# One first transfer, weights joined on VectorE in 16-bit steps, and a new order, in a convolution with two gated layers

## The chip, the cores and the metric

One core of one Trainium2 chip. The metric is the device time of one execution in microseconds; of several runs the median is given. TensorE is called PE, its weight load PEld, VectorE DVE, ScalarE ACT, GpSimd POOL, and the queue of SyncE, which issues most transfers, SP.

## The reference

The inputs are x (2 x 4096 x 192), eight rows of seven taps, and two pairs of matrices, 192 x 2048 and 2048 x 192.

```python
w = softmax(weight, -1)                       # 8 heads, 7 taps
x = causal_conv(x, w)                         # per head of 24 columns, over the sequence
h = x @ w_in                                  # first layer, 8192 x 192 @ 192 x 2048
P = a[0] + a[1] * h + a[2] * h2 + a[3] * h3
Q = 1.0 + np.abs(b[0]) * np.abs(h) + np.abs(b[1]) * h2
x = (P / (Q + 1e-06)) @ w_out
r = np.maximum(x @ w_in2, 0.0)                # second layer
out = (s * (r * r) + b2) @ w_out2
```

All of it is float32. The kernel keeps nearly float32 precision on PE by cutting operands into a high part (rounded to fp32r) and a low part (the remainder), with two or three products for one.

## The kernel before, in words

The 8192 tokens go in 16 blocks of 512, and the 2048 hidden columns in eight pairs of 128. For each block `x_path` convolves (`conv`, eight band matrices on PE), evacuates on ACT, transposes on PE and cuts the result into highs (ACT) and lows (DVE). `first` does one pair of the first layer: ten matmuls (`in1`, L383), then on ACT V, Q, R, Ln and Exp (L408 to L433), on DVE six steps (L419 to L450), on POOL one product (`lo`, L454), and on PE six and four matmuls (`out_high`, `out_low`, L392). `middle` turns the first layer's sums into the second's input, `second` does one pair of that layer (three steps on ACT, one on DVE, twenty matmuls), `finish` scales and stores. So a block has 8 pairs of each layer, and 8 `lo` products on POOL.

**Weights.** The matrices come as 64-bit integers (the float32 words, widened on the way in), 768 numbers wide and 16 tiles long: eight for the first layer, eight for the second. `load_raw` (L211, SP's queue) brings a tile of 767.8 KB. `convert` turns it into highs and lows:

- `masked` (DVE, L244) takes the sign off the top 16 bits, reading and writing every fourth 16-bit number
- `high` (ACT, L251) scales them into an integer tile z, `low` (ACT, L247) scales the lower word
- `sign` (DVE, L255) puts the sign back into every second 16-bit number of z
- `join` (POOL, L260) adds the two integer tiles, 768 wide, both in SBUF
- `highs` (ACT, L272 to L274) and `lows` (DVE, L278, L279, L282) cut the joined float into parts

**The start.** The taps come as 2 x 28 numbers (L670). Seven small steps on DVE and one on ACT make the softmax of them (L685 to L691), written with zeros around into one row per half of the heads. Eight transfers, four issued by SP and four by ACT (L697), spread that row into eight bands, 112 x 103 each, with a step of one number per partition. Coefficients a, b, s, b2 come in four further transfers on ACT's queue (L672, L702), each to 128 partitions. ACT's later instructions stand behind these issues in its own order. PE runs idle matmuls (`fill`, L659) meanwhile: 18 first, then 240 in the order, which must be done before block 0 of the second layer sums up.

**The order.** Every step is given to `Plan.order` with an engine, a cost, a due time (`when * PERIOD + KEY[name]`), the steps before it, and, for the steps marked `two` and for all of POOL, a lock that lets DVE and POOL not run at once. The planner picks for each engine the step of lowest due time among those that could start within WINDOW of the earliest. Steps are emitted in that order, so each engine and SP's queue has one fixed sequence; the waits between engines are semaphores.

Of the kernel before, what the change touches and what calls it, by code (L numbers as in the profile page):

```python
# [21 lines left out]
H, KS = 8, 7  # L22
# [16 lines left out]
PW = 3 * PC  # L39
VW = TR + TO - 1  # L40
MM = 0.2267
# [5 lines left out]

PERIOD = 29.4177
SAME, OTHER, WINDOW = 0.13, 0.18, 0.0816
KEY = {  # L50
    "B": -18.26, "Exp": 85.29, "Ln": 962.19, "S": -55.68, "Sq": 26.85, "V": -173.31,
    "add": -36.74, "again2": 92.78, "bias": -194.66, "conv": -113.91, "evac": -514.81,
    "f0": -183.70, "f1": -109.69, "fill": 1008.09, "finish": 1026.88, "flatten": 1223.69,
# [4 lines left out]
    "mid high": -118.59, "mid low": 106.79, "middle high": 7.19, "middle low": -60.45,  # L58
    "oh": 1243.60, "oh2": 1542.95, "ol": 20.35, "ol2": -329.62, "q": -163.53,
    "raw": -147.83, "relu": -68.11, "rest": -22.82, "rows": -471.89, "sign1": -269.27,  # L60
# [17 lines left out]
class Plan:  # L78
# [13 lines left out]
    def order(self):  # L92
# [23 lines left out]
        while len(out) < len(self.steps):  # L116
            first = None
            for engine, steps in ready.items():
                can = [(t, st) for t, st in ((start(st), st) for st in steps) if t is not None]
                if can:  # L120
                    t0 = min(t for t, _ in can)
                    t, st = min((c for c in can if c[0] <= t0 + WINDOW), key=lambda c: c[1].key)
                    if first is None or t < first[0]:
                        first = t, st
            t, st = first
            st.end = clock[st.engine] = t + st.cost
            if st.port:
                port[st.engine] = st.end
            if st.take:
                units = self.places[st.take]  # L130
                st.unit = min((u for u in units if units[u] is not None), key=units.get)
                units[st.unit] = None
            for holder in st.free:
                self.places[holder.take][holder.unit] = st.end
            ready[st.engine].remove(st)
            out.append(st)
            for d in users.get(st, ()):
                waits[d] -= 1
                if waits[d] == 0:
                    ready[d.engine].append(d)  # L140
# [4 lines left out]
def conv_rational_relu2(  # L145
    ctx: ExitStack,
    tc: tile.TileContext,
    xr: bass.AP,
    wr: bass.AP,
    w1: bass.AP,  # L150
    w2: bass.AP,
    a: bass.AP,
    b: bass.AP,
    s2: bass.AP,
    b2: bass.AP,
    out: bass.AP,
# [29 lines left out]
    ident = const.tile([P, P], F32, name="ident")  # L186
    band = const.tile([P, H, TO], F32, name="band")
    few = const.tile([P, 16], F32, name="few")
    ab, bb, babs, bias2 = few[:, 0:4], few[:, 4:6], few[:, 6:8], few[:, 8:10]
    ss, bs, lnb, exb, reb = (few[:, k:k + 1] for k in range(10, 15))  # L190
    ones = const.tile([P, 2], F32R, name="ones")
    qc = 1.0 + 1e-6

    def row(v):
        return bass.AP(v.tensor, v.offset, [[0, P], [1, v.shape[0]]])

# [34 lines left out]
    def convert(W, c, place, n, load):  # L231
# [8 lines left out]
        def masked(_):  # L240
            halves = raws[n].bitcast(U16).rearrange("p (n k) -> p n k", k=4)
            a["u"], a["top"] = halves[:, :, 3], halves[:, :, 2]
            a["y"] = raws[n].rearrange("p (n k) -> p n k", k=2)[:, :, 0]
            nc.vector.tensor_scalar(a["u"], a["top"], 0x7FFF, None, op0=ALU.bitwise_and)  # L244

        def low(_):
            nc.scalar.activation(a["y"], a["y"].bitcast(U32), AF.Copy, scale=2.0 ** -13)  # L247

        def high(tag):
            a["z"] = scratch(tag, I32, PW)  # L250
            nc.scalar.activation(a["z"], a["u"], AF.Relu, scale=2.0 ** 19, bias=reb)  # L251

        def sign(_):
            t = a["z"].bitcast(U16).rearrange("p (n k) -> p n k", k=2)[:, :, 1]
            nc.vector.scalar_tensor_tensor(  # L255
                t, a["top"], 0x8000, t, op0=ALU.bitwise_and, op1=ALU.bitwise_or
            )

        def join(_):
            nc.gpsimd.tensor_tensor(a["z"], a["z"], a["y"], op=ALU.add)  # L260

# [26 lines left out]

        s0 = st("masked", "DVE", 0.6, masked, (load,), two=True)
        s1 = st("low", "ACT", 0.8, low, (load, s0))  # L290
        s2 = st("high", "ACT", 0.85, high, (s0,), take="scratch")
        s3 = st("sign", "DVE", 0.93, sign, (s2,), two=True)
        s4 = st("join", "Pool", 1.84, join, (s1, s3))
        s5 = st("highs", "ACT", 1.35, highs, (s4, ("join", n - 1)))
        s6 = st("lows", "DVE", 1.05, lows, (s5,), two=True)
        st("weights", "DVE", 0.25, last_low, (s5, s6), free=(s2,), two=True)

# [12 lines left out]
    def x_path(blk):  # L310
# [339 lines left out]
    with tc.manual_schedule():  # L650
# [11 lines left out]

        fill(WARM)
        for n in range(FILLS):
            step("fill", n, "PE", 2 * MM, 0, lambda _: fill(2))

        small = tmp("Q", 3)[0:2].rearrange("p k n -> p (k n)")
        wt = small[:, 0:HH * KS].rearrange("p (h k) -> p h k", h=HH)
        mx = small[:, NB:NB + 3 * HH].rearrange("p (n h) -> p n h", h=HH)
# [21 lines left out]
        nc.vector.tensor_tensor(  # L691
            vv.rearrange("p (h n) -> p h n", h=HH)[:, :, TI - KS:TI],
            wt, each(mx[:, 2]), op=ALU.mult,
        )
        for h in range(H):
            v = vv[h // HH:h // HH + 1, h % HH * VW:(h % HH + 1) * VW]
            (nc.scalar, nc.sync)[h % 2].dma_start(  # L697
                out=band[:TR, h],
                in_=bass.AP(v.tensor, v.offset, [list(v.ap[0]), [1, TR], [1, TO]]),
            )  # L700
# [69 lines left out]
```

## Time and profile before

| | us |
|---|---|
| median of 3 runs | 1366.26 (1365.43 to 1367.29) |
| the profiled execution, its own time | 1367.33 |
| its span, first to last instruction | 1365.5 |
| PE busy | 1301.5 (95%) |
| DVE busy | 1222.5 (90%) |
| ACT busy | 1176.6 (86%) |
| POOL busy | 390.0 (29%) |

Busy time is a sum over stages that have different limits: PE's holds the idle matmuls of the start too. Which engine ends last is to be read stage by stage, from the view that cuts the span into stretches, and in the first 30 us from the timeline.

### The profile page before, as it was taken

How to read it: one execution, taken by the hardware profiler on the slowest of the kernel's cores; microseconds unless marked ns; L12 is line 12 of the kernel's file. 1: busy time of each engine (PE TensorE's matmuls, PEld its weight loads, DVE VectorE, ACT ScalarE, POOL GpSimd, SP SyncE). 2: the span in 40 equal slices, each digit the busy share in tenths (PEclk: the TensorE clock that was granted, in tenths of full speed). 3: DMA queues.
4: the chain of work that ended last, by engine and by line, in shares of the span. 5: the costliest groups of instructions: out<-in, count | busy, mean ns of one | idle time of the engine just before them, and what ended most of it. 6: DMA issues, size and time to landing. Idle time of an engine off the chain costs nothing.

```text
span 1365.5 us, 15251 instructions
## 1 busy us (share of the span) xinstructions
PE 1301.5 (95%) x5821; PEld 1033.7 (76%) x5830; DVE 1222.5 (90%) x1097; ACT 1176.6 (86%) x1270; POOL 390.0 (29%) x156
## 2 busy tenths in 40 slices
PE   8778589899999999999999999999999999999998
PEld 4445467677888888888888888888888888888776
DVE  3999999999998989999998989999998989899952
ACT  3766778798998989899998989899999989898965
POOL 1333342332323222222323323232323332222310
PEclk9898799999999999999999999999999999999999
DMA  6500000000101010000101010000001010000000
GB/s 152 225 24 23 17 5 0 21 13 1 32 0 33 0 33 1 21 12 0 33 0 32 1 33 0 21 12 10 23 1 32 0 33 1 20 0 5 12 16 12
DMA packets 12092, 31.16 MB, mean 23 GB/s; under 512 B 3124, under 2 KB 3124, under 8 KB 12020
## 3 DMA queue, kind: packets, MB, share of 16 engines
q1 hardware_dynamic: 10932, 30.01, 7.2%
q10 hardware_dynamic: 1088, 0.19, 0.3%
q8 instruction: 46, 0.75, 0.2%
q14 instruction: 26, 0.21, 0.1%
HBM read 19.46 MB, written 6.29 MB: 19 GB/s over the span
## 4 chain that ended last, share of the span: by engine, by line
PE 80%; DVE 13%; ACT 4%; issue 2%; DMA 1%; SPq 0%; ACTq 0%; DVEq 0%
PE h L383 39%; PE acc L392 38%; DVE Q L427 2%; PE h L317 1%; DVE Q L450 1%; DVE V L419 1%; DVE V L423 1%; DVE lo L544 1%; DVE hi L438 1%; DVE z L255 1%; DMA raw<-w 1%; DVE Q L444 1%; ACT V L408 1%; DVE raw L244 1%; DVE w L278 1%
## 5 line engine op out<-in xcount | busy, mean ns | idle before, releaser
L454 POOL TENSOR_TENSOR lo<-Q,R 128x1024 fp32r<-128x1024 f32 x128 | 347.0, 2711 | 832.0 <-DVE Q L450 461.9
L392 PE MATMUL acc<-hi,w 128*128 128x512 f32 x1536 | 388.9, 394 | 12.1 <-DVE hi L438 7.5
L392 PEld LDWEIGHTS acc<-hi,w 128*128 128x128 f32 x1536 | 288.8, 189 | 78.5 <-DVE hi L438 10.2
L392 PE MATMUL acc<-lo,w 128*128 128x512 f32 x1024 | 276.0, 396 | 5.5 <-POOL lo L454 4.9
L392 PEld LDWEIGHTS acc<-lo,w 128*128 128x128 f32 x1024 | 190.3, 189 | 49.4 <-POOL lo L454 5.8
L544 DVE TENSOR_TENSOR lo<-G,hi 128x1024 fp32r<-128x1024 f32 x128 | 166.1, 1297 | 33.9 <-PE acc L392 28.9
L408 ACT ACTIVATE V<-h,few 128x1024 f32<-128x1024 f32 x128 | 153.0, 1196 | 48.6 <-PE h L383 47.2
L383 PE MATMUL h<-x1h,w 128*128 128x512 f32 x512 | 166.6, 407 | 27.2 <-DVE x1s L355 12.9
L419 DVE TENSOR_TENSOR V<-V,h 128x1024 f32<-128x1024 f32 x128 | 155.2, 1212 | 34.8 <-ACT R L416 34.8
L533 ACT ACTIVATE G<-h 128x1024 f32<-128x1024 f32 x128 | 131.3, 1026 | 56.3 <-PE h L383 45.6
L427 DVE SCALAR_TENSOR_TENSOR Q<-Q,few,R 128x1024 f32<-128x1024 f32 x128 | 173.5, 1356 | 3.9 <-ACT R L416 3.7
L450 DVE SCALAR_TENSOR_TENSOR Q<-V,few,Q 128x1024 f32<-128x1024 f32 x128 | 168.2, 1314 | 0.3
L383 PE MATMUL h<-x2h,w 128*128 128x512 f32 x512 | 160.4, 395 | 6.5 <-DVE V L423 6.2
L430 ACT ACTIVATE R<-Q,few 128x1024 f32<-128x1024 f32 x128 | 146.1, 1141 | 23.5 <-DVE Q L427 23.2
L423 DVE SCALAR_TENSOR_TENSOR V<-V,few,h 128x1024 f32<-128x1024 f32 x128 | 163.4, 1276 | 2.7
L438 DVE SCALAR_TENSOR_TENSOR hi<-V,few,R 128x1024 fp32r<-128x1024 f32 x128 | 165.3, 1291 | 0.6 <-ACT R L433 0.3
L444 DVE SCALAR_TENSOR_TENSOR Q<-Q,hi 128x1024 f32<-128x1024 f32 x128 | 158.4, 1237 | 0.7
L433 ACT ACTIVATE R<-R,few 128x1024 f32<-128x1024 f32 x128 | 146.2, 1143 | 0.6
L537 ACT ACTIVATE hi<-G 128x1024 fp32r<-128x1024 f32 x128 | 136.0, 1063 | 8.2 <-PE acc L392 5.7
L416 ACT ACTIVATE R<-h,few 128x1024 f32<-128x1024 f32 x128 | 142.4, 1112 | 0.0
L383 PEld LDWEIGHTS h<-x1h,w 128*128 128x128 f32 x512 | 95.5, 192 | 55.9 <-issue 21.0
L540 ACT ACTIVATE G<-G 128x1024 f32<-128x1024 f32 x128 | 135.0, 1055 | 1.7
(79 smaller groups left out, 1660.8 us busy)
## 6 DMA issues: line engine op xcount, KB each, us to landing
raw<-w SPq DMA_DIRECT2D x16, 767.8 KB, 6.6
x_in<-xr SPq DMA_DIRECT2D x16, 420.0 KB, 3.8
out<-z SPq DMA_DIRECT2D x16, 256.0 KB, 2.2
x2d<-x2d SPq DMA_DIRECT2D x16, 128.0 KB, 2.2
out<-z SPq DMA_DIRECT2D x16, 128.0 KB, 2.3
x1d<-x1d SPq DMA_DIRECT2D x15, 128.0 KB, 2.7
band<-V SPq DMA_DIRECT2D x4, 45.1 KB, 9.6
band<-V ACTq DMA_DIRECT2D x4, 45.1 KB, 9.5
```

What stands on the lines that cost most here:

```text
L383: nc.tensor.matmul(h[:, k, :], lhsT=W[c][:, w + k * P:w + (k + 1) * P], rhs=x, start=terms is wide and n == 0, stop=terms is rest and n == ...
L392: nc.tensor.matmul(acc[:, m, :], lhsT=W[c][:, w + k * P:w + (k + 1) * P], rhs=x[:, k, :], start=terms is HIGH and c == 0 and k == 0 and n ...
L408: nc.scalar.activation(a["v"], a["h"], AF.Identity, bias=ab[:, 2:3], scale=ab[:, 3:4])
L419: nc.vector.tensor_tensor(a["v"], a["v"], a["h"], op=ALU.mult)
L423: nc.vector.scalar_tensor_tensor(v, v, ab[:, 1:2], a["h"], op0=ALU.add, op1=ALU.mult)
L427: nc.vector.scalar_tensor_tensor(q, q, babs[:, 1:2], a["r"], op0=ALU.mult, op1=ALU.add)
L433: nc.scalar.activation(a["r"], a["r"], AF.Exp, bias=exb, scale=-1.0)
L438: nc.vector.scalar_tensor_tensor(hi, a["v"], ab[:, 0:1], a["r"], op0=ALU.add, op1=ALU.mult)
L444: nc.vector.scalar_tensor_tensor(q, q, qc, a["hi"].bitcast(F32), op0=ALU.add, op1=ALU.mult)
L450: nc.vector.scalar_tensor_tensor(q, a["v"], ab[:, 0:1], q, op0=ALU.add, op1=ALU.subtract)
L454: nc.gpsimd.tensor_tensor(lo, a["q"], a["r"], op=ALU.mult)
L544: nc.vector.tensor_sub(lo, a["g"], a["hi"].bitcast(F32))
```

## The change

- `masked`, `high`, `sign` and POOL's `join` go. In their place: `top` (ACT) writes a shifted, positive copy of the top 16 bits into a dense 16-bit tile; `held` (DVE) clamps it between two constants into another dense tile; `left` (DVE) subtracts the two, dense; `join` (DVE) multiplies the difference by 8 and adds it into the upper 16 bits of z, every second number. `low` (ACT) now writes z itself.
- A raw tile is free after `low` of its tile (ACT), and no longer after POOL's `join`.
- Bands, taps and coefficients come as one tensor, 128 x 888 numbers, in one transfer on SP's queue ahead of x and the first raw tile. The bands hold the taps in their places and -3e38 elsewhere; softmax is done on them in place: on DVE a subtraction and a product per half of the heads (412 columns each), on ACT an Exp per half, beside the small steps on the taps (now 56 numbers on 112 partitions).
- PERIOD, WINDOW and all due times are new, the assumed lateness of the first transfers is 6.0 and 8.5 for 10.0 and 9.0, the 18 first idle matmuls are a step of the plan, and where two engines tie the planner emits POOL's step first.

```diff
 KEY, PERIOD, WINDOW: all numbers new (PERIOD 29.4177 to 16.9964, WINDOW 0.0816 to 0.0732)
+TOP, REB = 896.0 * 16, 18432.0
@@ Plan.order
-                    if first is None or t < first[0]:
+                    if first is None or (t, engine != "Pool") < (first[0], first[1].engine != "Pool"):
@@ convert
-        def masked(_):
-            ...
-            nc.vector.tensor_scalar(a["u"], a["top"], 0x7FFF, None, op0=ALU.bitwise_and)
-        def low(_):
-            nc.scalar.activation(a["y"], a["y"].bitcast(U32), AF.Copy, scale=2.0 ** -13)
-        def high(tag):
-            a["z"] = scratch(tag, I32, PW)
-            nc.scalar.activation(a["z"], a["u"], AF.Relu, scale=2.0 ** 19, bias=reb)
-        def sign(_):
-            ...
-        def join(_):
-            nc.gpsimd.tensor_tensor(a["z"], a["z"], a["y"], op=ALU.add)
+        def top(_):
+            t = wts.tile([P, 12 * PC], U16, tag=f"w{place}", name="top", bufs=1)
+            a["t"], a["c"] = t[:, 0:PW], t[:, PW:2 * PW]
+            numbers = raws[n].bitcast(I16).rearrange("p (n k) -> p n k", k=4)
+            nc.scalar.activation(a["t"], numbers[:, :, 2], AF.Relu, bias=reb)
+        def low(tag):
+            a["z"] = scratch(tag, I32, PW)
+            ...
+            nc.scalar.activation(a["z"], numbers[:, :, 0], AF.Copy, scale=2.0 ** -13)
+        def held(_):
+            nc.vector.tensor_scalar(
+                a["c"], a["t"], REB - TOP, REB + TOP, op0=ALU.max, op1=ALU.min
+            )
+        def left(_):
+            nc.vector.tensor_tensor(a["t"].bitcast(I16), a["t"], a["c"], op=ALU.subtract)
+        def join(_):
+            up = a["z"].bitcast(I16).rearrange("p (n k) -> p n k", k=2)[:, :, 1]
+            nc.vector.scalar_tensor_tensor(
+                up, a["t"].bitcast(I16), 8.0, up, op0=ALU.mult, op1=ALU.add
+            )
-        s4 = st("join", "Pool", 1.84, join, (s1, s3))
-        s5 = st("highs", "ACT", 1.35, highs, (s4, ("join", n - 1)))
+        s1 = st("top", "ACT", 0.94, top, (load, ("low", n - 1)))
+        s2 = st("low", "ACT", 0.86, low, (load, s1), take="scratch")
+        s3 = st("held", "DVE", 0.3, held, (s1,), two=True)
+        s4 = st("left", "DVE", 0.5, left, (s3,), two=True)
+        s5 = st("join", "DVE", 0.95, join, (s2, s4), two=True)
+        s6 = st("highs", "ACT", 1.35, highs, (s5,))
@@ the start
-        nc.sync.dma_start(out=wt, in_=wr)
-        for t, v in ((ab, a), (bb, b)):
-            nc.scalar.dma_start(out=t, in_=row(v))
+        nc.sync.dma_start(out=head, in_=first_rows)
         x_ins[0] = load_x(0)
         load_raw(0)
+        for h in halves:
+            t = band[:TR, h]
+            nc.vector.tensor_tensor(t, t, each(mx[:, 0, h], TO), op=ALU.subtract)
+            nc.scalar.activation(t, t, AF.Exp)
-        for h in range(H):
-            v = vv[h // HH:h // HH + 1, h % HH * VW:(h % HH + 1) * VW]
-            (nc.scalar, nc.sync)[h % 2].dma_start(out=band[:TR, h], ...)
-        for t, v in ((ss, s2), (bs, b2)):
-            nc.scalar.dma_start(out=t, in_=row(v))
+        for h in halves:
+            t = band[:TR, h]
+            nc.vector.tensor_tensor(t, t, each(mx[:, 2, h], TO), op=ALU.mult)
@@ the raw tiles
-                (("join", n - NPAIR),), late=2.0 if n else 9.0,
+                (("low", n - NPAIR),), late=2.0 if n else 8.5,
```

## Rows read from the trace of the kernel before

**Rows 1.** The stretches: us, each engine's busy us (instructions), PE clock, DMA share, GB/s.

```profile
20.00:210.00 190.00, 146.38 (x608) 97.88 (x617) 172.70 (x176) 136.38 (x189) 70.43 (x27) 0.88 0.20 71
210.00:350.00 140.00, 129.20 (x582) 103.77 (x582) 136.07 (x115) 119.75 (x127) 41.01 (x15) 0.98 0.05 12
...
600.00:1000.00 400.00, 400.00 (x1823) 328.06 (x1822) 371.67 (x329) 371.17 (x386) 113.72 (x42) 1.00 0.05 14
```

**Rows 2.** Timeline of the start: start us, duration us, engine, what, idle before.

```profile
0.74 0.37 SPq L670 DMA_DIRECT2D Q<-wr  x1
...
7.83 1.02 DVE L244 TENSOR_SCALAR raw<-raw 128x768 uint16<-128x768 uint16 x1 [4.27 <-DMA raw<-w]
...
18.93 0.20 ACT L703 ACTIVATE ones<-ident 128x2 fp32r<-128x2 f32 x1 [16.18 <-DMA band<-V]
...
20.40 0.66 PE L317 MATMUL h<-x_in,band 109*103 109x120 f32 x4 [1.29 <-DMA band<-V]
...
24.06 1.03 DVE L244 TENSOR_SCALAR raw<-raw 128x768 uint16<-128x768 uint16 x1 [2.88 <-DMA raw<-w]
...
26.43 0.81 PE L383 MATMUL h<-x1h,w 128*128 128x512 f32 x2
```

**Rows 3.** The chain that ended last, 0 to 150 us: start us, us, what.

```profile
11.82 12.22 DMA raw<-w
```

**Rows 4.** DMA issues of the page: KB each, median us to landing.

```profile
raw<-w SPq DMA_DIRECT2D x16, 767.8 KB, 6.6
x_in<-xr SPq DMA_DIRECT2D x16, 420.0 KB, 3.8
```

**Rows 5.** ACT groups by shape, 20 to 210 us: busy us, mean ns, idle before.

```profile
L251 ACT ACTIVATE z<-raw,few 128x768 int32<-128x768 uint16 x16 | 15.9, 997 | 12.8 <-DVE w L282 8.4 <-DVE raw L244 4.3
...
L247 ACT ACTIVATE raw<-raw 128x768 int32<-128x768 uint32 x16 | 14.6, 911 | 0.0
...
L272 ACT CAST w<-z 128x512 fp32r<-128x512 f32 x15 | 9.1, 608 | 1.1 <-POOL z L260 1.1
...
L273 ACT CAST w<-z 128x128 fp32r<-128x128 f32 x15 | 4.5, 297 | 0.0
```

**Rows 6.** DVE's timeline: gaps from one start to the next.

```profile
24.89 0.91 DVE L278 TENSOR_TENSOR w<-z,w 128x512 fp32r<-128x512 f32 x2
25.83 0.29 DVE L279 TENSOR_TENSOR w<-z,w 64x128 fp32r<-64x128 f32 x1
26.15 0.69 DVE L354 TENSOR_TENSOR x1l<-h,x1h 128x512 fp32r<-128x512 f32 x1
26.76 0.67 DVE L355 TENSOR_TENSOR x1s<-h,x1d 64x512 fp32r<-64x512 f32 x1
...
46.71 1.06 DVE L255 SCALAR_TENSOR_TENSOR z<-raw,z 128x768 uint16<-128x768 uint16 x1
47.66 1.26 DVE L423 SCALAR_TENSOR_TENSOR V<-V,few,h 128x1024 f32<-128x1024 f32 x1
```

**Rows 7.** POOL's timeline: a join.

```profile
28.53 1.90 POOL L260 TENSOR_TENSOR z<-z,raw 128x768 int32<-128x768 int32 x1 [5.35 <-DVE z L255]
```

**Rows 8.** DVE's timeline beside POOL: stretched steps.

```profile
28.75 2.57 DVE L244 TENSOR_SCALAR raw<-raw 128x768 uint16<-128x768 uint16 x1
...
57.61 3.20 DVE L255 SCALAR_TENSOR_TENSOR z<-raw,z 128x768 uint16<-128x768 uint16 x1
...
202.61 2.78 DVE L450 SCALAR_TENSOR_TENSOR Q<-V,few,Q 128x1024 f32<-128x1024 f32 x1
...
209.25 2.38 DVE L282 TENSOR_TENSOR w<-z,w 64x128 fp32r<-64x128 f32 x1
```

**Rows 9.** DVE groups by shape, 20 to 210 us, with and without matmul's tile.

```profile
L427 DVE SCALAR_TENSOR_TENSOR Q<-Q,few,R 128x1024 f32<-128x1024 f32 x12 | 19.1, 1588 | 3.6 <-ACT R L416 3.5
...
L419 DVE TENSOR_TENSOR V<-V,h 128x1024 f32<-128x1024 f32 x12 | 14.7, 1227 | 1.6 <-ACT R L416 1.6
```

**Rows 10.** The same group, 600 to 1000 us.

```profile
L427 DVE SCALAR_TENSOR_TENSOR Q<-Q,few,R 128x1024 f32<-128x1024 f32 x43 | 54.8, 1275 | 0.0
```

More of the change, by code (lines that the diff above doesn't have):

```diff
@@ L16 @@
 U16 = mybir.dt.uint16
+I16 = mybir.dt.int16
 AF = mybir.ActivationFunctionType
@@ L39 @@
 PW = 3 * PC
-VW = TR + TO - 1
+LEAST = -3e38
+NBAND, NTAP = H * TO, H * KS
 MM = 0.2267
@@ L46 @@
 HIGH, LOW = ((PC, 0), (NH + PC, 0), (O1, 1)), ((PC, 0), (O1, 1))
-PERIOD = 29.4177
-SAME, OTHER, WINDOW = 0.13, 0.18, 0.0816
+PERIOD = 16.9964
+SAME, OTHER, WINDOW = 0.13, 0.18, 0.0732
 KEY = {
-    "B": -18.26, "Exp": 85.29, "Ln": 962.19, "S": -55.68, "Sq": 26.85, "V": -173.31,
-    "add": -36.74, "again2": 92.78, "bias": -194.66, "conv": -113.91, "evac": -514.81,
-    "f0": -183.70, "f1": -109.69, "fill": 1008.09, "finish": 1026.88, "flatten": 1223.69,
[4 rows of a table removed]
-    "mid high": -118.59, "mid low": 106.79, "middle high": 7.19, "middle low": -60.45,
-    "oh": 1243.60, "oh2": 1542.95, "ol": 20.35, "ol2": -329.62, "q": -163.53,
-    "raw": -147.83, "relu": -68.11, "rest": -22.82, "rows": -471.89, "sign1": -269.27,
[3 rows of a table removed]
+    "B": 102.33, "Exp": 1175.83, "Ln": 1019.08, "S": 1195.94, "Sq": 1114.55, "V": 1064.40,
+    "add": -118.57, "again2": -113.73, "bias": 925.80, "conv": 12.58, "evac": -157.54,
+    "f0": 90.25, "f1": -152.71, "fill": 1057.49, "finish": 1148.84, "flatten": 14.26,
[4 rows of a table added]
+    "mid high": -78.15, "mid low": -3.35, "middle high": -235.38, "middle low": -102.48,
+    "oh": 1088.61, "oh2": 1257.68, "ol": 911.43, "ol2": 11.63, "q": -155.55, "raw": 34.25,
+    "relu": 1117.17, "rest": 987.03, "rows": -233.55, "store": -133.50, "store2": -119.63,
[3 rows of a table added]
 }
@@ L186, in conv_rational_relu2 @@
     ident = const.tile([P, P], F32, name="ident")
-    band = const.tile([P, H, TO], F32, name="band")
+    head = const.tile([P, NBAND + NTAP + 8], F32, name="head")
+    band = head[:, 0:NBAND].rearrange("p (h n) -> p h n", h=H)
+    wt = head[0:TR, NBAND:NBAND + NTAP].rearrange("p (h k) -> p h k", h=H)
+    given = head[:, NBAND + NTAP:]
+    ab, bb, ss, bs = given[:, 0:4], given[:, 4:6], given[:, 6:7], given[:, 7:8]
     few = const.tile([P, 16], F32, name="few")
-    ab, bb, babs, bias2 = few[:, 0:4], few[:, 4:6], few[:, 6:8], few[:, 8:10]
-    ss, bs, lnb, exb, reb = (few[:, k:k + 1] for k in range(10, 15))
+    babs, bias2 = few[:, 0:2], few[:, 2:4]
+    lnb, exb, reb = (few[:, k:k + 1] for k in range(4, 7))
     ones = const.tile([P, 2], F32R, name="ones")
     qc = 1.0 + 1e-6
-    def row(v):
-        return bass.AP(v.tensor, v.offset, [[0, P], [1, v.shape[0]]])
     def load_x(blk):
@@ L238, in convert @@
         a = {}
[L240 to L254 removed]
+        def top(_):
[4 more added lines that the diff above has]
+        def low(tag):
+            a["z"] = scratch(tag, I32, PW)
+            numbers = raws[n].bitcast(U32).rearrange("p (n k) -> p n k", k=2)
+            nc.scalar.activation(a["z"], numbers[:, :, 0], AF.Copy, scale=2.0 ** -13)
[7 more added lines that the diff above has]
+            up = a["z"].bitcast(I16).rearrange("p (n k) -> p n k", k=2)[:, :, 1]
             nc.vector.scalar_tensor_tensor(
[L256 removed]
+                up, a["t"].bitcast(I16), 8.0, up, op0=ALU.mult, op1=ALU.add
             )
[L259 to L260 removed]
         def highs(_):
@@ L287, in st @@
             return step(name, n, engine, cost, n, run, after, kind=name + m, **kw)
[L289 to L292, printed above, removed]
-        s4 = st("join", "Pool", 1.84, join, (s1, s3))
-        s5 = st("highs", "ACT", 1.35, highs, (s4, ("join", n - 1)))
-        s6 = st("lows", "DVE", 1.05, lows, (s5,), two=True)
-        st("weights", "DVE", 0.25, last_low, (s5, s6), free=(s2,), two=True)
+        s1 = st("top", "ACT", 0.94, top, (load, ("low", n - 1)))
[4 more added lines that the diff above has]
+        s6 = st("highs", "ACT", 1.35, highs, (s5,))
+        s7 = st("lows", "DVE", 1.05, lows, (s6,), two=True)
+        st("weights", "DVE", 0.22, last_low, (s6, s7), free=(s2,), two=True)
     def x_tiles(n):
@@ L360, in x_path @@
         ld = step("x load", blk, "DMA", 2.5, when, load if blk else None, (("tr", blk - 1),),
-                  late=2.0 if blk else 10.0)
+                  late=2.0 if blk else 6.0)
         cv = step("conv", blk, "PE", 1.65, when, conv, (ld,), take="slot")
@@ L661, in fill, with each @@
                 )
-        fill(WARM)
+        warm = step("warm", 0, "PE", 8.0, 0, lambda _: fill(WARM))
         for n in range(FILLS):
[L665 to L669, printed above, removed]
-        nc.sync.dma_start(out=wt, in_=wr)
-        for t, v in ((ab, a), (bb, b)):
-            nc.scalar.dma_start(out=t, in_=row(v))
+            step("fill", n, "PE", 2 * MM, 0, lambda _: fill(2), (warm,))
+        mx = tmp("Q", 3)[0:TR, 0, 0:3 * H].rearrange("p (n h) -> p n h", h=H)
+        nc.sync.dma_start(out=head, in_=first_rows)
         x_ins[0] = load_x(0)
         load_raw(0)
-        nc.gpsimd.memset(reb, -896.0 * 2.0 ** 23)
+        nc.gpsimd.memset(reb, REB)
         make_identity(nc, ident)
-        vv = tmp("V", 3)[0:2].rearrange("p k n -> p (k n)")[:, 0:HH * VW]
-        nc.vector.memset(vv, 0.0)
         for t in (*rests[1], *rests[2]):
             nc.gpsimd.memset(t[D1:P].bitcast(F32), 0.0)
-        def each(v):
-            return bass.AP(v.tensor, v.offset, [list(v.ap[0]), [1, HH], [0, KS]])
+        def each(v, n=KS):
+            return bass.AP(v.tensor, v.offset, [list(v.ap[0]), [1, v.shape[1]], [0, n]])
         nc.vector.tensor_reduce(mx[:, 0], wt, axis=mybir.AxisListType.X, op=ALU.max)
@@ L690, in conv_rational_relu2 @@
         nc.vector.reciprocal(mx[:, 2], mx[:, 1])
[L691 to L694, printed above, removed]
-        for h in range(H):
-            v = vv[h // HH:h // HH + 1, h % HH * VW:(h % HH + 1) * VW]
[L697 to L700, printed above, removed]
-        for t, v in ((ss, s2), (bs, b2)):
-            nc.scalar.dma_start(out=t, in_=row(v))
+        for h in halves:
+            t = band[:TR, h]
+            nc.vector.tensor_tensor(t, t, each(mx[:, 2, h], TO), op=ALU.mult)
         nc.scalar.activation(ones, ident[:, 0:2], AF.Copy, bias=1.0, scale=0.0)
@@ L741 @@
     at = np.arange(0, S, NB)[:, None, None] + at
+    bands = np.full((P, H, TO), LEAST, weight.dtype)
+    for k in range(KS):
+        t = np.arange(TO)
+        bands[TI - 1 - k - t, :, t] = weight[:, k]
+    rest = np.concatenate([v.reshape(-1) for v in (weight, moe_a, moe_b, moe2_s, moe2_b)])
+    first_rows = np.concatenate([bands.reshape(P, NBAND), np.tile(rest, (P, 1))], 1)
     def words(w_in, w_out):
@@ L751 @@
     arrays = {
+        "first_rows": first_rows,
         "xr": xpad[:, at].transpose(0, 1, 2, 4, 3, 5).reshape(NBLK, TR, H * NTI * G),
-        "wr": weight[:, ::-1].reshape(2, HH, KS),
         "w1": words(moe_w_in, moe_w_out), "w2": words(moe2_w_in, moe2_w_out),
-        "a": moe_a, "b": moe_b, "s2": moe2_s, "b2": moe2_b,
     }
```

7 lines of the change are left out of this document (2 added, 5 removed), and 14 rows, old and new, of the table KEY.

## The prediction

> **What bounds the kernel now.** I read the stretches of the span first, because PE's 95% mixes stages and holds idle matmuls [rows 1]. From 600 to 1000 us PE is busy 400 of 400 us: there only PE's own work counts, and the change adds and removes none. From 20 to 210 us PE is at 146 of 190 us, part of it idle matmuls, and DVE at 172.7 of 190, while ACT has 136 and POOL 70. From 210 to 350 us DVE is at 136.1 of 140 and PE still loses 10.8. So the opening is set by DVE, which converts sixteen weight tiles beside the first layer of block 0, and the reader is to look for DVE's time there. PE's clock is 0.88 in that stretch, but DVE ends last, so a full clock would give nothing there.
>
> Next I read the start in order of time [rows 2]. The first raw tile is there at 7.83, but ACT, behind its share of the band transfers, does its first work at 18.93, PE's convolution waits for bands until 20.40, and the first product of the first layer starts at 26.43. In the chain of waits one piece is longest: the second raw tile, issued behind the bands on SP at 11.82, takes 12.22 us to land [rows 3]. From 24.06 on, when DVE takes that tile, it hardly stops. What DVE has done by 24.06 is therefore worth its full length later.
>
> Last I looked for what stretches DVE's steps. An L244 of 1.03 us takes 2.57 when POOL's join starts 0.2 us ahead of it [rows 2, 7, 8]. L427, with two inputs in SBUF, means 1588 ns in 20 to 210 us and 1275 ns later, when L419, which reads a matmul's tile and only one tile of SBUF, means 1227 [rows 9, 10]. So a DVE step that begins beside a POOL step waits for it.
>
> **The start: -10 us.** The new first transfer is 128 x 888 x 4 = 455 KB, issued where the taps' was, at 0.74 [rows 2]. The nearest rows are x's 420 KB with 3.8 us and a raw tile with 6.6 [rows 4]; I take 3.8, the nearer size, with the whole queue free: it lands at 4.5. Then come eight small steps at some 0.2 us, as L703 takes [rows 2], together 1.6, and on DVE four wide ones of 412 columns: between the 0.32 us from start to start of 128 columns (25.83 to 26.15) and 0.61 of 512 (26.15 to 26.76), so 0.53 by a straight line [rows 6], 2.1 together. The two Exp on ACT lie mostly beside them. Bands at about 8.3 for 20.40; with 6.6 and 0.61 it is 11.4. ACT issues no transfer any more.
>
> Raw tile 0 now stands behind 455 KB more. Before, 1188 KB (x and the tile) were there 7.1 us after 0.74, 6 us per MB; so it comes 2.7 later, at 10.5. From there to 24.06 are 13.6 us. ACT needs per weight 1.00 + 0.91 + 0.61 + three times 0.30 = 3.4 us [rows 5], with `top` priced as L251, same input, and `low` as L247; x's path costs it about five copies like L272's 0.61, 3 us. So (13.6 - 3) / 3.4 = 3.1 weights are through by 24.06. Each is 3.55 us on DVE (1.97, below, plus the lows: 0.94 + 0.32 + 0.32 [rows 6]), so 11.0; with 1.2 for x's two lows it is 12.2. Before, DVE had done 1.02 + 1.05 = 2.1 by then. The lead is 10.1; I take 10. Bounds: 7, if bands come at 11.4, and 12.2, the whole wait for tile 1 [rows 3]. The later raw tiles, with no bands ahead on SP, are not late at 6 us per MB (4.6 us each, against 3.55 on DVE and 3.4 on ACT plus the pairs).
>
> **POOL's joins: -18.6 us.** Sixteen joins go. In DVE's timeline thirteen steps beside one are stretched, first L244 at 28.75 (2.57 for 1.03), last L450 at 202.61 (2.78 for 1.28) [rows 8]; over their kind's undisturbed time the thirteen add up to 18.6 us, on the engine that ends last. Nothing takes the place of a join on POOL. Four of the eleven `lo` products there also stretch a step, by 8.5 together (first L255 at 57.61, 3.20 for 1.05, last L282 at 209.25, 2.38 for 0.28 [rows 8]); these I leave. Lower bound: half, 9, where DVE would now wait for ACT, which has 54 us free in 190 [rows 1]; upper: 18.6 + 8.5 = 27.
>
> **DVE's steps per weight: +3 us.** What counts is start to start: L244 0.83 (24.06 to 24.89), L255 0.95 (46.71 to 47.66) [rows 2, 6], together 1.78. The new join has L255's form, width and stride: 0.95. For `held` and `left`, dense 16-bit, no row exists. At one column per step as now they cost 0.83 and 0.95; at no cost per column they keep the 0.32 of the shortest row. By bytes 768 such numbers are 384 words, which the straight line above puts at 0.51 each; I take this, nearest to what is moved. So 0.95 + 1.02 = 1.97, 0.19 more than before, times 16 is 3. Bounds: 1.59, -3 in all, to 2.73, +15.
>
> The Trainium skill, "VectorE: DVE Perf Modes", section "The perf-mode tier table", says that dense 16-bit data in SBUF runs at four numbers per cycle in tensor_scalar and two in tensor_tensor; with its table of fixed cycles I estimate 0.26 and 0.46 us. By that rule this term would be -1.8 and the time 1335.9; no row before shows a dense 16-bit step.
>
> **Costed at nothing.** `top` for `high` and the new `low`: same lengths on ACT, under DVE's time. Raw tiles freed by ACT and not by POOL: they come earlier, but the only wait of DVE for a tile after the first is the 2.88 us ahead of 24.06 [rows 2]. The idle matmuls: PE has the room. What POOL loses: it was at 70 of 190 us. On SP, x's second block and the raw tiles move past four bands, all counted above. The due times of all steps are new; where PE is full I cost the new order at nothing, its cover being 5.4 us of free time per block on DVE: 28.3 us idle over 42 `lo`, so 5.25 blocks [rows 1]. If that is used up, PE starves.
>
> **Sum.** -10 - 18.6 + 3 = -25.6 us. The profiled execution took 1367.33 (its span 1365.5), so 1341.7; the median of the runs stands 1.07 lower, so 1340.7. What is late next is still DVE in the opening, then PE.
>
> **Rivals.**
> - *Dense steps run no faster than strided ones.* +15.2 for +3: 1352.9. For it: not one fast row. Against it: nothing but bytes. 0.12.
> - *Only the start counts.* DVE's freed time turns into waits for ACT, since a weight now goes ACT, DVE, ACT, DVE with three dependent steps in between: 1340.7 + 18.6 = 1359.3. For it: 17.3 us of DVE's 190 are waits already [rows 1]. Against it: ACT is at 72%. 0.12.
> - *The order also frees the rest.* No `lo` stretches DVE in the opening (8.5) and PE loses nothing from 210 to 350 (10.8 [rows 1]): 1321.4. 0.10.
> - *Slower: `lo` collides where PE is full.* Every such collision costs DVE about 2.1 us (8.5 / 4). From 600 to 1000 us there is none, as L427's mean shows [rows 10]; an order of other due times can bring them back. DVE's slack holds 2.5 of the 8 per block; at four of eight, DVE is 3.1 us per block too long, and over 13 blocks that is 40: 1381. It eats the whole gain from 3.5 of 8. For it: in the opening 4 of 11 collided under the same planner. Against it: the planner locks the two engines against each other. The Trainium skill, "GPSIMD Engine Reference", section "Key points", puts such waits down to VectorE steps in a two-port mode or with two SBUF inputs; L427 and L419 agree, but L244, with one input, was stretched too [rows 8]. By that rule the new weights bring three such steps for two, each open to a `lo`. 0.08.
> - *No effect*, if some step I hold for covered ends last: 0.03.
>
> **How the numbers follow.** The forecast has 0.55; its own range, from the bounds of the start and the dense steps' lower half, is 1332 to 1347. The range reaches to the low rival and to the start alone, 1322 to 1359; outside are the slower case, no effect, and about half of each edge case, 0.2 in all. A difference of 0.2%, 2.7 us, is about what a measurement of this kernel can tell. Faster: 0.55 + 0.12 + 0.12 + 0.10 = 0.89, less 0.01 for edges, 0.88; same 0.03; slower 0.09.
>
> **What would show it.** Right: ACT's first weight step near 10.5, the convolution near 8.5, the first product before 17; no DVE step over 2 us outside a `lo`; `held` and `left` near 0.5; DVE still over 90% busy from 20 to 180 us, PE full from about 325 on and 100% after. Wrong: DVE idle over 30 us in the opening (the start alone), steps of 0.8 and more (no fast mode), or L427's mean above 1.4 us after 400 us with PE below 97% (the slower case). I would also be wrong if the last weight but one got its L282, at 209.25 before [rows 8], less than 20 us earlier.

## The result, and the profile after

The changed kernel takes 1312.09 us (median of four runs, 1311.70 to 1312.66) where the kernel before took 1366.74 beside it: a ratio of 0.9602, 95% interval 0.9585 to 0.9618. That is 54.7 us less. I had forecast 25.6 less, 1340.7, and the time lies 10 us below the range. The direction was right, and something as large as the whole forecast was left out. Of the runs below, one execution of the start alone took 2627 us, and its number there leaves that one out.

The stretches of the changed kernel's span, in the columns of [rows 1]:

```profile
0.00:20.00 20.00, 17.46 (x96) 10.57 (x96) 11.36 (x26) 12.40 (x24) 2.33 (x12) 1.00 0.62 223
20.00:210.00 190.00, 170.36 (x765) 116.12 (x764) 183.77 (x218) 166.21 (x212) 46.30 (x16) 0.97 0.16 57
210.00:350.00 140.00, 139.56 (x638) 114.49 (x638) 131.77 (x116) 128.31 (x134) 39.16 (x15) 1.00 0.06 16
350.00:600.00 250.00, 250.00 (x1150) 205.76 (x1149) 237.60 (x208) 232.50 (x244) 66.80 (x27) 1.00 0.05 14
600.00:1000.00 400.00, 399.89 (x1831) 328.21 (x1830) 377.65 (x329) 370.75 (x387) 108.69 (x43) 1.00 0.06 17
```

PE is full from 210 us on, where it lost 10.8 of 140 us before, and nothing changed where it was full already. In the opening DVE is free for 6.2 of 190 us, 17.3 before. Of its busy time less is waiting too: summed over DVE's timeline from 20 to 210 us, each step against the shortest of its kind (called its stretching below), 17 steps were stretched by 27.3 us before and one is by 2.0 now. From 210 to 350 us it is 8.7 before and 2.0 now.

The start, from the timeline, in the columns of [rows 2]:

```profile
1.19 5.93 PE L664 MATMUL acc<-G 128*128 128x512 bf16 x20 [1.19 <-DVE G L659]
...
4.14 0.21 DVE L685 TENSOR_REDUCE Q<-head 112x8 f32<-112x56 f32 x1 [3.01 <-DMA head<-first_rows]
...
6.95 1.85 PE L322 MATMUL h<-x_in,head 109*103 109x120 f32 x16
...
8.61 0.99 ACT L246 ACTIVATE top<-raw,few 128x768 uint16<-128x768 int16 x1 [2.24 <-DMA raw<-w]
...
14.76 0.81 PE L388 MATMUL h<-x1h,w 128*128 128x512 f32 x2
```

The first transfer is there by 4.14 (forecast 4.5), the convolution starts at 6.95 (8.3), the first weight at 8.61 (10.5), the first product at 14.76 (before 17), 11.7 us earlier than before. The first line matters below: 20 idle matmuls stand ahead of the convolution.

DVE's groups by shape in 20 to 210 us, which answer to [rows 9], and three gaps from its timeline, which answer to [rows 6]:

```profile
L432 DVE SCALAR_TENSOR_TENSOR Q<-Q,few,R 128x1024 f32<-128x1024 f32 x18 | 23.0, 1280 | 0.1
...
L424 DVE TENSOR_TENSOR V<-V,h 128x1024 f32<-128x1024 f32 x18 | 21.9, 1216 | 0.2
...
L263 DVE SCALAR_TENSOR_TENSOR z<-top,z 128x768 int16<-128x768 int16 x14 | 14.5, 1038 | 0.9 <-ACT z L251 0.7
...
L259 DVE TENSOR_TENSOR top<-top 128x768 int16<-128x768 uint16 x14 | 7.7, 551 | 0.2
...
L254 DVE TENSOR_SCALAR top<-top 128x768 uint16<-128x768 uint16 x14 | 5.0, 355 | 2.2 <-ACT top L246 2.2
```

```profile
28.46 0.34 DVE L254 TENSOR_SCALAR top<-top 128x768 uint16<-128x768 uint16 x1
28.73 1.27 DVE L428 SCALAR_TENSOR_TENSOR V<-V,head,h 128x1024 f32<-128x1024 f32 x1
...
29.92 0.54 DVE L259 TENSOR_TENSOR top<-top 128x768 int16<-128x768 uint16 x1
30.39 0.88 DVE L283 TENSOR_TENSOR w<-z,w 128x512 fp32r<-128x512 f32 x2
...
38.49 1.02 DVE L263 SCALAR_TENSOR_TENSOR z<-top,z 128x768 int16<-128x768 int16 x1
39.40 1.22 DVE L424 TENSOR_TENSOR V<-V,h 128x1024 f32<-128x1024 f32 x1
```

L432 (L427 before) means 1280 ns and no longer 1588, as undisturbed in [rows 10] (1275). From start to start `held` takes 0.27, `left` 0.47 and `join` 0.91, 1.65 per weight for 1.78.

### The profile page after: what moved, and what is told of

Its sections match the earlier page's. It is cut to its first block, busy times and chain, and to the rows that moved or that the text cites. A ratio compares the mean times of both kernels' runs of the same rounds, so it can differ in the third digit from the quotient of the medians.

```text
span 1310.3 us, 15275 instructions
## 1 busy us (share of the span) xinstructions
PE 1281.9 (98%) x5830; PEld 1023.5 (78%) x5830; DVE 1202.4 (92%) x1115; ACT 1178.1 (90%) x1272; POOL 336.7 (26%) x140
## 4 chain that ended last, share of the span: by engine, by line
PE 87%; DVE 8%; ACT 3%; issue 1%; DMA 1%; POOL 0%; ACTq 0%; SPq 0%; DVEq 0%; POOLq 0%
PE acc L397 42%; PE h L388 42%; PE h L322 2%; DVE V L428 1%; DVE V L424 1%; DVE Q L432 1%; DVE z L263 1%; DVE hi L443 1%; DVE Q L449 1%; DVE Q L455 1%; DVE w L283 1%; DMA raw<-w 1%; PE h L342 0%; DVE top L259 0%; PE h L343 0%
## 5 line engine op out<-in xcount | busy, mean ns | idle before, releaser
L459 POOL TENSOR_TENSOR lo<-Q,R 128x1024 fp32r<-128x1024 f32 x128 | 334.4, 2613 | 922.8 <-PE acc L397 388.4
L397 PE MATMUL acc<-lo,w 128*128 128x512 f32 x1024 | 270.0, 392 | 7.7 <-POOL lo L459 7.6
L443 DVE SCALAR_TENSOR_TENSOR hi<-V,head,R 128x1024 fp32r<-128x1024 f32 x128 | 177.3, 1385 | 33.3 <-PE acc L397 30.4
L549 DVE TENSOR_TENSOR lo<-G,hi 128x1024 fp32r<-128x1024 f32 x128 | 156.7, 1225 | 28.7 <-PE acc L397 25.4
L413 ACT ACTIVATE V<-h,head 128x1024 f32<-128x1024 f32 x128 | 153.0, 1195 | 15.1 <-PE h L388 14.7
L455 DVE SCALAR_TENSOR_TENSOR Q<-V,head,Q 128x1024 f32<-128x1024 f32 x128 | 165.4, 1292 | 0.8
L432 DVE SCALAR_TENSOR_TENSOR Q<-Q,few,R 128x1024 f32<-128x1024 f32 x128 | 163.6, 1278 | 2.6 <-ACT R L421 2.2
L428 DVE SCALAR_TENSOR_TENSOR V<-V,head,h 128x1024 f32<-128x1024 f32 x128 | 163.2, 1275 | 2.6
L449 DVE SCALAR_TENSOR_TENSOR Q<-Q,hi 128x1024 f32<-128x1024 f32 x128 | 156.9, 1226 | 0.6
L417 ACT ACTIVATE Q<-h 128x1024 f32<-128x1024 f32 x128 | 130.0, 1016 | 29.9 <-POOL lo L459 29.8
L421 ACT ACTIVATE R<-h,head 128x1024 f32<-128x1024 f32 x128 | 142.3, 1112 | 0.1
```

The costliest lines, as they stand in the source:

```text
L397: nc.tensor.matmul(acc[:, m, :], lhsT=W[c][:, w + k * P:w + (k + 1) * P], rhs=x[:, k, :], start=terms is HIGH and c == 0 and k == 0 and n ...
L413: nc.scalar.activation(a["v"], a["h"], AF.Identity, bias=ab[:, 2:3], scale=ab[:, 3:4])
L428: nc.vector.scalar_tensor_tensor(v, v, ab[:, 1:2], a["h"], op0=ALU.add, op1=ALU.mult)
L432: nc.vector.scalar_tensor_tensor(q, q, babs[:, 1:2], a["r"], op0=ALU.mult, op1=ALU.add)
L443: nc.vector.scalar_tensor_tensor(hi, a["v"], ab[:, 0:1], a["r"], op0=ALU.add, op1=ALU.mult)
L449: nc.vector.scalar_tensor_tensor(q, q, qc, a["hi"].bitcast(F32), op0=ALU.add, op1=ALU.mult)
```

## The experiments

The change has three parts: the start (S), the weights' steps (W) and the order (O). The first six runs put them on and off. The order of a kernel is kept by leaving its plan as it is, step by step and cost by cost, and changing only what a step emits; so a run "in the old order" has the planner's sequences of before, engine by engine. Ratios are to the kernel before, run beside them. Its medians there lie between 1364.66 and 1366.74 us, so a difference between two rows is good to about 2 us.

| parts | us | ratio, 95% interval |
|---|---|---|
| S | 1358.69 | 0.9951 (0.9938 to 0.9964) |
| W | 1356.64 | 0.9935 (0.9914 to 0.9957) |
| S, W | 1357.18 | 0.9941 (0.9923 to 0.9958) |
| O | 1351.07 | 0.9899 (0.9885 to 0.9914) |
| O, S | 1339.62 | 0.9817 (0.9802 to 0.9832) |
| O, W | 1324.62 | 0.9702 (0.9685 to 0.9720) |
| O, S, W (the changed kernel) | 1312.09 | 0.9602 (0.9585 to 0.9618) |

**The parts in the old order.** S alone: the kernel before, with the new first transfer and softmax.

```diff
-        nc.sync.dma_start(out=wt, in_=wr)
+        nc.sync.dma_start(out=head, in_=first_rows)
...
-            (nc.scalar, nc.sync)[h % 2].dma_start(out=band[:TR, h], ...)
```

> The order and the weights' steps of before, with only the new first transfer (bands, taps, coefficients at once, softmax on the bands). Theory A, each part brings its own time on DVE whatever the order is: the convolution can begin at 6.95 instead of 17.48 and 20.40 us, the first product came 11.7 us earlier in the changed kernel, so about -12 us, 1355. Theory B, the new order is what lets the parts count, and in the old sequence each engine waits for the next late thing: about -5 us, 1362.

W alone: the kernel before, with the new steps in the old places.

```diff
-        s2 = st("high", "ACT", 0.85, high, (s0,), take="scratch")
-        s3 = st("sign", "DVE", 0.93, sign, (s2,), two=True)
-        s4 = st("join", "Pool", 1.84, join, (s1, s3))
+        s2 = st("high", "ACT", 0.85, lambda tag: (top(0), low(tag), held(0), left(0)), (s0,),
+                take="scratch")
+        s3 = st("sign", "DVE", 0.93, join, (s2,), two=True)
+        s4 = st("join", "Pool", 1.84, None, (s1, s3))
```

> The order and the start of before, with only the new weight steps, put in the places of the old ones (top, low, held and left where high stood, join where sign stood, nothing on POOL). Theory A: no join stretches DVE any more (18.6 us), the dense steps give 1.8, and a weight's chain is some 2 us shorter, together -27 us, 1340. Theory B: DVE's freed time turns into waits, since DVE still takes weights and pairs in the old turn: about -10 us, 1357. DVE's stretched steps beside POOL fall from 17 to about 4 by both.

S and W: both edits.

> The order of before with the new start and the new weight steps. Theory A: -12 and -27 add, about 1328, and the new order is worth the remaining 16 us. Theory B: about -19 us, 1348, and the new order is worth 36.

S alone gave 7.0 us, between A and B; W alone 9.0, as B has it; and the two together 8.5, no more than W alone and less than B's 19. Theory A, and with it the sum of my prediction, which let each part bring its own time, fell here; of B the direction stood.

**The parts in the new order.** O, W: the changed kernel with the old start (the first diff turned round). O, S: the changed kernel with the old steps in the new places. O alone: both.

> The new order and the new weight steps with the start of before (bands by eight transfers, coefficients by four). Theory A: the start's 12 us come back on top of 1312, so 1324. Theory B: DVE catches up within the opening because the order leaves it room, so about 1317.

```diff
-        s1 = st("top", "ACT", 0.94, top, (load, ("low", n - 1)))
-        s2 = st("low", "ACT", 0.86, low, (load, s1), take="scratch")
+        s1 = st("top", "ACT", 0.94, masked, (load, ("low", n - 1)))
+        s2 = st("low", "ACT", 0.86, lambda tag: (high(tag), low(0)), (load, s1), take="scratch")
...
-        s5 = st("join", "DVE", 0.95, join, (s2, s4), two=True)
+        s5 = st("join", "DVE", 0.95, lambda _: (sign(0), join(0)), (s2, s4), two=True)
```

> The new order and the new start, with the old weight steps in the places of the new ones (masked at top, high and low at low, sign and POOL's join at join). Theory B1, the sequence itself is the gain, because DVE takes the second layer's weights and the pairs in another turn: near 1335, the joins' stretching alone (18.6 us and a little) on top of 1312. Theory B2, the sequence fits only the steps it was planned for, since the planner did not know of a join on POOL there: 1350 or more.

> The new order with the old start and the old weight steps. B1: 12 us more than the run with the new order and the new start and the old steps, so near 1347, still 19 under before. B2: no better than before, 1366 or more.

In the new order the start is worth 12.5 us (1324.62 to 1312.09) or 11.5 (1351.07 to 1339.62), and the weights 27.5 (1339.62 to 1312.09) or 26.5 (1351.07 to 1324.62): there the parts add. So with O and W theory A held (1324), and B's 1317 fell. The order alone brings 14 us with the old steps, which it was not planned for, so it lay between B1 and B2: B1's distances were right and both times 4 us higher. With both parts present the order is worth 45 (1357.18 to 1312.09). The next runs ask what in the old order kept the parts down.

What the weights' 27.5 us are made of can be read from the two runs with O and S, without and with W. But for the weights' own steps DVE does the same 205 steps in both, in the same order, up to its eighth `lo<-G,hi` (the last of block 0's second layer), and there the whole difference is already present (246.1 to 218.6 us), first without W, then with it:

```profile
244.85 1.21 DVE L546 TENSOR_TENSOR lo<-G,hi 128x1024 fp32r<-128x1024 f32 x1
```

```profile
217.44 1.21 DVE L549 TENSOR_TENSOR lo<-G,hi 128x1024 fp32r<-128x1024 f32 x1
```

Summed over DVE's timeline up to there, stretching falls from 23.3 us (17.0 beside a join, 6.2 beside `lo` alone) to 2.0, DVE's idle time from 17.7 to 13.7, and its undisturbed steps take 2.2 less.

**Idle matmuls ahead of the convolution.** PE's timeline of the run with S and W in the old order, where the bands were there as early as in the changed kernel:

```profile
1.19 16.28 PE L665 MATMUL acc<-G 128*128 128x512 bf16 x61 [1.19 <-DVE G L660]
17.30 1.81 PE L323 MATMUL h<-x_in,head 109*103 109x120 f32 x16
```

The old plan expected late bands and put 61 idle matmuls first, as the kernel before did:

```profile
1.19 16.46 PE L659 MATMUL acc<-G 128*128 128x512 bf16 x61 [1.19 <-DVE G L654]
```

Two runs leave 42 of them out, which takes them out of the work (the new order does them later).

```diff
-            step("fill", n, "PE", 2 * MM, 0, lambda _: fill(2))
+            step("fill", n, "PE", 2 * MM, 0, (lambda _: fill(2)) if n > 20 else None)
```

> The order of before with the new start, and 42 of the 240 idle matmuls left out, those that stand first in PE's sequence. In the run with the new start alone the convolution still began behind 61 idle matmuls, at 17.3 us; in the new order 20 stand there. Theory C: PE's sequence hid the new start; without them the start is worth its 12 us, so 1354. Rival: the rest of the old sequence swallows it too, and the time stays at 1359.

> The order of before with both new parts, and the same 42 idle matmuls left out. C: from 1357 down by what the start brings, 10 to 12 us, so about 1346. Rival, the old sequence swallows it: 1357.

Measured: 1352.05 (ratio 0.9906, 0.9892 to 0.9921) with S, 13 us under before, and 1347.44 (0.9875, 0.9859 to 0.9891) with S and W. So C held: the start's time was there, and PE's own sequence hid about half of it with the old steps (7.0 of 13.1 came through) and all of it with the new ones (1356.64 with W, 1357.18 with S and W). With S and W the convolution and the first product now come where the changed kernel has them:

```profile
7.16 1.89 PE L323 MATMUL h<-x_in,head 109*103 109x120 f32 x16 [0.18 <-DVE head L698]
...
14.80 0.82 PE L389 MATMUL h<-x1h,w 128*128 128x512 f32 x2
```

What came back is DVE's waiting: up to its eighth `lo<-G,hi` it is busy for 195 us in both of the runs with S and W and idles 9.6 us less without the 42 (27.8 for 37.4). A run that does them later, in place of leaving them out, was not made.

**The weights' place.** In the run with W alone DVE's idle time ahead of `held` looked large, and I put it down to my placing, not to the order. DVE's group in 20 to 210 us:

```profile
L254 DVE TENSOR_SCALAR top<-top 128x768 uint16<-128x768 uint16 x16 | 5.7, 358 | 27.6 <-ACT top L246 27.6
```

```diff
-        s2 = st(..., lambda tag: (top(0), low(tag), held(0), left(0)), ...)
-        s3 = st("sign", "DVE", 0.93, join, (s2,), two=True)
+        s2 = st(..., lambda tag: (top(0), low(tag)), ...)
+        s3 = st("sign", "DVE", 0.93, lambda _: (held(0), left(0), join(0)), (s2,), two=True)
```

> As the run with both parts in the old order and the 42 idle matmuls left out, but held and left stand on DVE in front of join, in the old place of sign, and no longer right behind top's place. In the run with the new weights alone DVE waited 27.6 us for top, sixteen times just issued. Theory D: that place, mine and not the old order's, swallowed the weights' gain; with it mended both parts bring their 12 and 27 us, so about 1327, and the new order is worth the 15 us it has alone. Rival B: the old turn of weights and pairs itself holds them back, so still over 1340.

Measured 1344.76 (0.9852, 0.9837 to 0.9867): only 2.7 us less, and D fell. Its 27.6 us were misread: 16.8 of them are one wait at the start, before the first `held`, which the place has nothing to do with, and the other eight waits make 10.8.

```profile
20.29 0.36 DVE L254 TENSOR_SCALAR top<-top 128x768 uint16<-128x768 uint16 x1 [16.82 <-ACT top L246]
```

With the place mended DVE idled 16.2 us instead of 20.6 from 20 to 210 us, but its stretched steps grew from 12.4 to 16.7 us. So 32.7 us between the two orders stayed.

**POOL's `lo` beside DVE.** Between 20 and 350 us DVE's steps are stretched by 23 us in that run and by 4 in the changed kernel. Two runs cut `lo` on POOL to 32 of its 1024 columns, which leaves the rest of the low part of the first layer's output at zero; all products then write into one tile.

```diff
-            nc.gpsimd.tensor_tensor(lo, a["q"], a["r"], op=ALU.mult)
+            nc.gpsimd.tensor_tensor(lo[:, :, 0:16], a["q"][:, :, 0:16], a["r"][:, :, 0:16], op=ALU.mult)
```

> As the run with both parts in the old order, idle matmuls and places mended (1345), with lo on POOL cut from 1024 to 32 of its columns (the rest of the low part is left at zero), so that POOL hardly holds DVE. Theory E, collisions: the 23 us of stretched steps between 20 and 350 us go, about 1322. Rival F, the turn of weights and pairs: DVE's steps are short again but wait as long, about 1340.

> The changed kernel with lo cut in the same way. It has 4 us of stretched steps between 20 and 350 us, so by both theories 1308 to 1310; with E the two sequences then differ by about 14 us, with F by about 30.

Measured: 1319.84 (0.9670, 0.9654 to 0.9686) in the old order, 24.9 us less, and 1308.78 (0.9590, 0.9576 to 0.9604) in the new one, 3.3 us less. The two orders now differ by 11.1 us, so E holds in the main: some 22 of the 32.7 us were `lo` colliding with DVE (19 us more of stretching in the old order). The short `lo` also takes POOL's own time off the way to `out_low`, but in the old order PE's matmuls waited for `lo` only 2.7 us from 20 to 350 us with the full product and 0.9 with the short one. L433 in 20 to 350 us, first in the old order with full `lo`, then with the short one:

```profile
L433 DVE SCALAR_TENSOR_TENSOR Q<-Q,few,R 128x1024 f32<-128x1024 f32 x30 | 44.7, 1489 | 4.3 <-ACT R L422 4.1
```

```profile
L433 DVE SCALAR_TENSOR_TENSOR Q<-Q,few,R 128x1024 f32<-128x1024 f32 x33 | 42.2, 1278 | 1.5 <-ACT R L422 1.3
```

Of the last 11 us some may be waits: DVE idles 16.9 of 190 us in the old order with short `lo` and 6.4 in the new, by the stretches of the two runs:

```profile
20.00:210.00 190.00, 164.72 (x724) 116.00 (x731) 173.14 (x209) 158.57 (x209) 8.14 (x15) 0.93 0.15 54
```

```profile
20.00:210.00 190.00, 171.73 (x763) 117.49 (x773) 183.62 (x219) 167.21 (x213) 12.03 (x16) 0.96 0.16 57
```

I did not divide them further.

**The rule on ties.** The changed kernel without it:

```diff
-                    if first is None or (t, engine != "Pool") < (first[0], first[1].engine != "Pool"):
+                    if first is None or t < first[0]:
```

> The changed kernel without the rule that puts POOL's step first where two engines tie; all due times stay. The planner's sequences differ from the changed kernel's from the first pairs on. If the due times carry the gain, within 5 us of 1312; if the rule is what keeps lo beside steps that read a matmul's tile, DVE's stretched steps come back, some 2 us each, and it is 1320 or more.

Measured 1399.61, slower than before (1.0255, 1.0240 to 1.0270), 87 us over the changed kernel. The stretch from 600 to 1000 us in the columns of [rows 1]:

```profile
600.00:1000.00 400.00, 381.22 (x1720) 311.51 (x1719) 372.01 (x309) 349.46 (x363) 118.21 (x40) 0.99 0.05 14
```

DVE's group by shape in 350 to 1000 us:

```profile
L432 DVE SCALAR_TENSOR_TENSOR Q<-Q,few,R 128x1024 f32<-128x1024 f32 x65 | 93.7, 1442 | 8.4 <-ACT R L421 8.3
```

And one place in the timeline of POOL and DVE (start, duration):

```profile
501.52 2.90 POOL L459 TENSOR_TENSOR lo<-Q,R 128x1024 fp32r<-128x1024 f32 x1 [5.37 <-PE acc L397]
...
502.19 3.31 DVE L449 SCALAR_TENSOR_TENSOR Q<-Q,hi 128x1024 f32<-128x1024 f32 x1
```

PE is at 381 where it was full, and DVE's steps are stretched beside `lo` again, by 42 us from 350 to 1000 us (8 in the changed kernel). The due times carry nothing by themselves: they give a fast sequence together with the rule, and one slower than before without it. Between the rule's two sides DVE, ACT, PE and SP all get other sequences, so this run does not price the rule alone, and the old due times with the rule were not run.

**The price of a join, and of dense steps.** Both on the changed kernel, same order.

```diff
+            a["spare"] = t[:, 2 * PW:4 * PW].bitcast(I32)
...
+            nc.gpsimd.tensor_tensor(a["spare"], a["z"], a["z"], op=ALU.add)
```

> The changed kernel with one more POOL addition, 128 x 768 integers, behind each of the sixteen joins; its result is used by nothing, but the highs wait until it is done, as they waited for POOL's join before. The order stays. If the joins' price is the stretching of DVE that I took (18.6 us), 1331; if the new order can place it beside steps that read a matmul's tile, under 1320; if the longer chain of a weight counts too, over 1340.

Measured 1335.50 (0.9784, 0.9767 to 0.9800): 23.4 us, between the first figure (the joins' stretching) and the third (the longer chain). The groups in 20 to 210 us show both, POOL's addition and the highs on ACT that wait for it:

```profile
L267 POOL TENSOR_TENSOR top<-z 128x768 int32<-128x768 int32 x15 | 33.0, 2197 | 76.4 <-DVE z L264 69.3 <-issue 7.1
...
L279 ACT CAST w<-z 128x512 fp32r<-128x512 f32 x15 | 9.2, 617 | 24.1 <-POOL top L267 24.1
```

DVE's stretched steps come to 16.5 us in that stretch, 14.5 more than in the changed kernel; DVE's waits grow by about 10. In this run POOL's step stands behind the join on DVE, so a weight has one step more in its chain than in either kernel.

```diff
-            a["t"], a["c"] = t[:, 0:PW], t[:, PW:2 * PW]
+            pairs = t[:, 0:2 * PW].rearrange("p (n k) -> p n k", k=2)
+            a["t"], a["c"] = pairs[:, :, 0], pairs[:, :, 1]
```

> The changed kernel with the 16-bit tiles of top, held and left spread to every second number instead of dense; same order, same sums. At the prices of strided steps (0.83 and 0.95 us from start to start for 0.27 and 0.47) DVE has 16 times 1.04 = 17 us more: 1329 if DVE ends last all through the weights; less, some 1318, if waits swallow it.

Measured 1321.83 (0.9687, 0.9672 to 0.9701), 9.7 us more. The groups of `left` and `held` in 20 to 210 us:

```profile
L260 DVE TENSOR_TENSOR top<-top 128x768 int16<-128x768 uint16 x14 | 14.9, 1067 | 0.2
L255 DVE TENSOR_SCALAR top<-top 128x768 uint16<-128x768 uint16 x14 | 8.6, 612 | 2.4 <-ACT top L247 2.4
```

`left` is 0.52 us longer and `held` 0.26, together 0.77, times 16 is 12.4 us on DVE: most of it reaches the end.

## Why the prediction was wrong, point by point

- **What bounds the opening** was right: DVE is at 97% from 20 to 210 us after the change too, and time taken off it comes back at the end. PE's granted clock there rose from 0.88 to 0.97 without a term of mine, and no run sets it apart.
- **The start, -10 us:** right in size, 9.2 to 13.1 us wherever PE's sequence lets it through (my 455 KB are 444 in the unit of the rows, worth 0.1 us). Wrong was a sentence among those costed at nothing, that PE has the room for the idle matmuls. In the old order 61 of them stand ahead of the convolution; I saw PE wait for bands at 20.40 [rows 2] and not what ended right before.
- **POOL's joins, -18.6 us, and DVE's steps, +3:** together -15.6, measured 26.5 to 27.5 less in the new order. The joins' stretching was right in size, 17.0 us there; the other terms are 4.2 of `lo`'s stretching, which I left, 4.0 of DVE's waits, which I had at nothing, and the 2.2 of the next point. The addition put back behind the new join costs more, 23.4, because about 10 of it are waits.
- **The dense steps** were mis-sized (the +3 above): 0.27 and 0.47 us from start to start, not 0.51 each, so the term is near -2 us (1.65 for 1.78, times 16) and not +3. The page I quoted, the Trainium skill's "VectorE: DVE Perf Modes", section "The perf-mode tier table", gave 0.26 and 0.46 by my estimate; the trace agrees. The rival of slow dense steps falls with it.
- **The order, costed at nothing,** is the step that failed. I looked for what the new due times could do where PE is full, and there they do nothing; for the opening I gave no reason at all. They bring 14 us with the old start and steps and 45 with the new, and by DVE's last step of block 1's second layer all of it is there (349.6 to 334.4 us, and 339.7 to 294.5). I also let both parts bring their time without asking whether the old sequence would have let them through; in it they bring 8.5 us together. Of the 45, 9.7 are idle matmuls out of the way (1357.18 to 1347.44), 2.7 my placing of the weights' steps, and 32.7 the rest, of which the runs with short `lo` put some 22 on collisions of POOL and DVE. What keeps the last 11 apart stays open. Of the forecast's own bounds, the upper end of 1347 does not follow from those it names: they give 1343.7.
- **The rivals.** "The order also frees the rest", 1321.4, named the mechanism (no `lo` stretches DVE, PE full from 210 us), and I gave it 0.10. The 8.5 us of `lo` that the sum said "these I leave" were the wrong choice. "Only the start counts" fell for the changed kernel: DVE waits less, not more. In the old order its mechanism was there: with both parts DVE idles 23.4 us from 20 to 210 us (17.3 before), and the time is 1357.18, near that rival's 1359.3. The slower case is real as a mechanism: without the rule on ties the same kernel takes 1399.6, by the collisions where PE is full that I priced at 1381. The rule decides between the two, and I had it among the edits without a price.
- **What would show it:** the first product, the dense steps and PE at 100% came as written or better; PE is full by 210 us, over 100 us earlier than I wrote, and DVE's last but one weight got its last step 48 us earlier (209.25 before [rows 8]):

```profile
161.19 0.29 DVE L287 TENSOR_TENSOR w<-z,w 64x128 fp32r<-64x128 f32 x1
```

## What to carry to other kernels

A kernel whose engines run in a sequence planned ahead must be judged as one thing: here two parts that are worth 12 and 27 us gave 8.5 together in the sequence planned for the old durations, because work planned as filler, and steps planned beside other steps, stood in the way. So when a change replaces the order too, price it by what the old order spends on waits and on engines that hold each other, and not by the parts alone: from 20 to 350 us DVE was stretched by 36 us and idle for 21 before, by 4 and for 14.5 after, and these 39 us with the start's 12 come near the 54.7. The two views to read for that are the queue of each engine up to its first useful work, and the mean of one group of instructions in the stage that matters against the same group in an undisturbed one.

## What the runs showed of the hardware that I had not expected

Spread to every second number, `held` takes 0.61 us for 768 numbers (0.36 dense), where L244, reading and writing every fourth, took 1.03 [rows 2]. I had given the spread form L244's price; as L244 does another operation too, no run tells what of the distance is the stride. A step of DVE with one input in SBUF waits for POOL as well: L244 took 2.57 beside a join [rows 8], and the dense `held`, in the old order with the place mended, 2.53 beside a `lo`:

```profile
39.25 3.27 POOL L460 TENSOR_TENSOR lo<-Q,R 128x1024 fp32r<-128x1024 f32 x1 [36.21 <-ACT top L246]
40.21 2.53 DVE L254 TENSOR_SCALAR top<-top 128x768 uint16<-128x768 uint16 x1
```

The Trainium skill's "GPSIMD Engine Reference", section "Key points", names a two-port mode or two SBUF inputs for such waits; the stretched L427, L432 and L449 have two. L244 and `held` have one, so by that sentence they would run in a two-port mode; no run shows their mode.
